# Five moves in the attention stage and one in the feed-forward stage of a fused kernel

## The chip, the cores and the metric

The kernel runs on one core of a Trainium2 chip. The metric is the device time of one execution in microseconds (us). The engines are TensorE (PE, with its weight loads as PEld), VectorE (DVE), ScalarE (ACT), GpSimd (POOL) and SyncE (SP, which here only issues DMAs). Each engine works through a queue of its own in order; semaphores tie the queues together.

## The reference

Three layers in float32: a linear attention with a decaying state, a gated top-1 mixture of experts with a skip, and a feed-forward layer.

```python
# attention: B, H, S, D = 4, 8, 768, 48
for t in range(S):
    state = alpha[:, :, t, :, None] * state + einsum('bhd,bhe->bhde', k[:, :, t], v[:, :, t])
    y[:, :, t] = einsum('bhd,bhde->bhe', q[:, :, t], state)
# mixture of experts: N = 3072 tokens, D = 384, E = 8 experts, F = 1024
do = x @ w_skip > 0
e = argmax(x[do] @ w_gate); gate = softmax(x[do] @ w_gate)[e]
out[do] = x[do] + gate * (relu(x[do] @ w1[e]) @ w2[e])
# feed-forward: d_ff = 2048
h = out @ w_in
return (h - tanh(h)) @ w_out
```

## The kernel before, in words

**Attention.** The sequence is cut into 24 units u (6 chunks of 128 steps for each of 4 batch entries, the batch entry running fastest). For each unit VectorE makes two scans over the decays `it`: `F` (running product from the start of the chunk, `scanF`, L196) and `G` (the same from its end, `scanG`, L203). `scanF` ends with a reciprocal that writes the four initial values of `G` into a tile `d1s[u % 2]` in SBUF, which is zero elsewhere; `scanG` reads that tile as its second operand. Then `qh` = q times F on GpSimd (L209), `kh` = k times G on VectorE (L214), and `pf`, a few factors for the state, on GpSimd (L221). TensorE makes the scores `pa` (`mmA`, L229; one PSUM buffer of two banks), VectorE masks them into `am` (`mask`, L234), and TensorE makes `py` from the state (`mmYs`) and from `am` (`mmYa`), transposes `kh` (`trk`) and updates the state (`mmS`). `evx`, `mmX` and `evxa` transpose the result into rows and compute the nine logits.

The order is written by hand. `astep(s)` issues, for step s: the loads of units s+4 and s+3, `mmA(s)`, `evx(s-2)`, the scans and `qh`, `pf` of unit s+2, `mmYs(s-1)`, `trk(s)`, `mmX(s-2)`, `mask(s)`, `mmYa(s-1)`, then `scanG` and `kh` of unit s+2, then whatever the lists `at[s]` and `aft[s]` hold, and `mmS(s)`. So scans run two units ahead of the scores.

**Routing.** The tokens are routed in three batches of 12, 8 and 4 units. For batch c, `route1` (argmax and so on, 13 small VectorE operations) and `route2` (counts by matmul, at the end of the step) come two steps after the batch's last unit, and `evr` and `route3` (the row addresses `loc`) one step later. Then `scatter(u)` writes the rows of one unit to DRAM (`xb`) with an indirect DMA of GpSimd: two in each of steps 15 to 20 for the first batch. `rload(0)` (issued at step 21) reads the first 512 token rows back.

**Weights.** A float32 weight tile is split into two parts for TensorE by `wsplit`. For the feed-forward weights that is four pieces, s0 (two VectorE operations), s1 (one VectorE, two ScalarE), s2 (two VectorE) and s3 (one VectorE). Five of them (NE0) are split during the attention steps, four steps apart, and the last five (NLATE) in the feed-forward loop itself: the pieces of weight k in steps 2k, 2k, 2k+1, 2k+1, all ahead of the step's own work.

**After the attention.** A tail routes the last batch and starts the feed-forward of the first 512 tokens on the five early weights (`mm1b`: h, then tanh, g, gh, gl; `mm2b`: y, two steps behind). Then 64 expert steps, then the feed-forward loop: 11 steps that finish the first 512 tokens with the remaining weights, and 80 steps for the other five blocks.

Of the kernel before, what the change touches and what calls it, by code (L numbers as in the profile page):

```python
# [9 lines left out]
F32 = mybir.dt.float32  # L10
# [51 lines left out]
def tile_kernel(ctx: ExitStack, tc: tile.TileContext, att0, att, vt, wsg, wmoe, wff, out):  # L62
# [47 lines left out]
    def flat(t_):  # L110
        return t_.rearrange("p a t -> p (a t)")
# [80 lines left out]
    def scanF(u):  # L192

        d = U[u]
        d["F"] = w2.tile([PR, NP, C], F32, tag="F", name=f"F{u}")
        V.tensor_tensor_scan(flat(d["F"]), d["it"][:, :NP * C], flat(ind), 0.0, ALU.mult, ALU.add)  # L196
        V.reciprocal(d1s[u % 2][:, :, C - 1:C], d["F"][:, :, C - 1:C])

    def scanG(u):

        d = U[u]
        d["G"] = w2.tile([PR, NP, C], F32, tag="G", name=f"G{u}")
        V.tensor_tensor_scan(flat(d["G"])[:, ::-1], d["it"][:, 1:NP * C + 1][:, ::-1], flat(d1s[u % 2])[:, ::-1], 0.0,  # L203
                             ALU.mult, ALU.add)

    def mkqh(u):
        d = U[u]
        d["qh"] = w2.tile([PR, NP, C], F32, tag="qh", name=f"qh{u}", bufs=4)
        G.tensor_tensor(d["qh"], d["qq"], d["F"], ALU.mult)  # L209

    def mkkh(u):
        d = U[u]
        d["kh"] = w2.tile([PR, NP, C], F32, tag="kh", name=f"kh{u}", bufs=3)
        V.tensor_tensor(d["kh"], d["kk"], d["G"], ALU.mult)  # L214

    def mkpf(u):
        d = U[u]
# [68 lines left out]
    def evx(u):  # L286
        d = U[u]
        d["xT"] = rt.tile([PR, NP, C], F32, tag="xT", name=f"xT{u}")
        A.copy(d["xT"], d["py"])

    def mmX(u):

        d = U[u]
        d["px"] = ps["T"].tile([128, NP, 128], F32, tag=f"X{u % 2}", name=f"px{u}")
        for p in range(NP):
            T.matmul(d["px"][:, p, :XW], d["xT"][:, p], selw[:, p], start=p == 0, stop=p == NP - 1)  # L296

    def evxa(u):
        k, i = where[u]
        r, n = RT[k], BATCHES[k]  # L300
        if i == 0:
            r["xr"] = rt.tile([128, n, RW], F32, name=f"xr{k}", bufs=1)
            r["l4"] = rt.tile([128, n, NP, 9], F32, name=f"l4{k}", bufs=1)
        A.copy(r["xr"][:, i, :DM].rearrange("p (a d) -> p a d", a=NP), U[u]["px"][:, :, :PD])
        A.copy(r["l4"][:, i], U[u]["px"][:, :, PD:XW])


    RT = [dict() for _ in BATCHES]
# [300 lines left out]
    ind = w1.tile([PR, NP, C], F32, name="ind")  # L609
    G.memset(ind, 0.0)  # L610
    G.memset(ind[:, :, 0:1], 1.0)
    d1s = [w1.tile([PR, NP, C], F32, name=f"d1_{i}") for i in range(2)]
    for t_ in d1s:
        V.memset(t_, 0.0)
    warm = cp.tile([128, 2], F32, name="warm")
    V.memset(warm, 1.0)
    A.activation(warm, warm, AF.Exp)
# [13 lines left out]
    zero = w1.tile([128, RW], F32, name="zero")  # L631
    scanF(0)
    mkqh(0)
    mkpf(0)
    scanG(0)
    mkkh(0)
    for t_ in pys:
        V.memset(t_, 0.0)
    G.memset(zero, 0.0)
# [19 lines left out]
    cnt4 = cp.tile([128, 1], F32, name="cnt4")  # L659
    scanF(1)  # L660
    mkqh(1)
    mkpf(1)
    scanG(1)
    mkkh(1)
    aload(2)
    for u in range(3):
        vload(u)
# [19 lines left out]
            xb[r0:r0 + 512, :].rearrange("(a p) d -> p a d", a=4), zero.unsqueeze(1).to_broadcast([128, 4, RW])))  # L687
    for k in range(NE0):
        at[max(1, 4 * k)].append(lambda k=k: wload(NMU + k))
        for s, f_ in zip((3 - k // 4, 4, 4, 6), wsplit(NMU + k)):  # L690
            aft[4 * k + s].append(f_)
    at[21].append(lambda: rload(0))
    for i in range(BATCHES[0]):
        aft[15 + i // 2].append(lambda i=i: scatter(i))

    def astep(s):

        def ok(u):
            return 0 <= u < NU

        def pX_(name):
            return ps["T"].tile([128, 512], F32, tag=f"X{s % 2}", name=name)

        if ok(s + 4):
            aload(s + 4)
        if ok(s + 3):
            vload(s + 3)
        for f_ in at[s]:
            f_()
        mmA(s)  # L710
        if ok(s - 2):
            evx(s - 2)
        c1 = next((k for k in range(len(BATCHES)) if s == first[k] + BATCHES[k] + 2), None)
        c3 = next((k for k in range(len(BATCHES)) if s == first[k] + BATCHES[k] + 3), None)
        if c3 is not None:
            evr(c3)
        if c1 is not None:
            route1(c1)
        if ok(s + 2):
            scanF(s + 2)  # L720
            mkqh(s + 2)
            mkpf(s + 2)
        if ok(s - 1):
            mmYs(s - 1)
        trk(s)
        if ok(s - 1):
            evst(s - 1)
        evk(s)
        if ok(s - 2):
            mmX(s - 2)  # L730
            evxa(s - 2)
        mask(s)
        if ok(s - 1):
            mmYa(s - 1)
        if c1 is not None:
            route1b(c1)
        if c3 is not None:
            route3(c3)
        if ok(s + 2):
            scanG(s + 2)  # L740
            mkkh(s + 2)
        for f_ in aft[s]:
            f_()
        mmS(s)
        if c1 is not None:
            route2(c1, pX_)
# [4 lines left out]
    ip_ctx.close()  # L751
    p0 = pool("p0", 1)
    rings["x2", 0] = p0
    for s in (NU - 2, NU - 1):
        a = 2 * (s - NU + 2)
        aft[s].append(lambda a=a: split2(0, a))
        astep(s)
        split2(0, a + 1)


    def pX(name):
        return ps["T"].tile([128, 512], F32, tag="X0", name=name)

    last = len(BATCHES) - 1
    mmYs(NU - 1)
    mmYa(NU - 1)
    evx(NU - 2)
    mmX(NU - 2)
    evxa(NU - 2)
    evx(NU - 1)  # L770
    att_ctx.close()
    rings["raw"] = pool("raws", 3, route_ctx, "right")
    part = p0.tile([128, 4, DM], F32, name="part")
    blk0 = ExitStack()
    rings["g"] = pool("g0", 3, blk0)
    i0, a0 = mm1b(0, 0, psS)
    i0(4)
    for u in range(first[1], first[last]):
        scatter(u)
    mmX(NU - 1)  # L780
    evxa(NU - 1)
    i0()
    for i in range(RING0):
        wload(i)
# [10 lines left out]
    evr(last)  # L795
    route1b(last)
    route3(last)
    for u in range(first[last], NU):
        scatter(u)
    psT_ctx.close()  # L800
# [50 lines left out]
    for e in range(1, NE):  # L851
        for a in range(2):
            aft[NF * e - 4 + a].append(lambda e=e, a=a: xprep(e, a))
        if e + 1 < NE:
            at[NF * e - 1].append(lambda e=e: xload(e + 1))
    at[20].append(lambda: rload(1))
    for i in range(NMU + 4):
        for f_ in at[i]:
            f_()
        if i < NMU:  # L860
            mm1(i)
        if 2 <= i < NMU + 2:
            mm2(i - 2)
        for f_ in aft[i]:
            f_()
# [3 lines left out]
    rings["x2", 1] = pool("p1", 1, ff_ctx, "right")  # L869
    rings["g"] = pool("g1", 2, ff_ctx, "right")  # L870
    steps = [(nb, f) for nb in range(NU // 4) for f in range(NF2) if nb or f >= NE0]
    at, aft = collections.defaultdict(list), collections.defaultdict(list)
    for k in range(NLATE):
        r = NMU + NF2 - NLATE + k
        at[max(0, 2 * k - 1 + 1)].append(lambda r=r: wload(r))
        for n, f_ in zip((0, 0, 1, 1), wsplit(r)):
            at[2 * k + n].append(f_)
    for nb in range(1, NU // 4):
        i = steps.index((nb, 0))
        for a in range(4):  # L880
# [4 lines left out]
    for i in range(len(steps) + 1):  # L885
        for f_ in at[i]:
            f_()
        if i < len(steps):
            issue, after = mm1b(*steps[i])
            issue()  # L890
            collections.deque(after(), 0)
        if 2 <= i < len(steps):
            mm2b(*steps[i - 2])
        elif i == len(steps):
            mm2b(steps[-1][0], *(f for _, f in steps[-2:]))
        for f_ in aft[i]:
            f_()
# [128 lines left out]
```

## Time and profile before

| what | value |
|---|---|
| median of 3 runs | 739.13 us (737.74 to 741.64) |
| the profiled execution | 738.44 us, of which the span of the profile is 736.8 us |
| attention with its last row copies | about 8 to 158 us |
| tail with the early feed-forward | about 158 to 181 us |
| expert steps | about 181 to 324 us |
| feed-forward on the late weights | about 324 to 379 us |
| the rest of the feed-forward | about 379 to 737 us |
| TensorE busy | 686.1 us (93%) |
| VectorE busy | 449.8 us (61%) |
| GpSimd busy | 125.3 us (17%) |

The times are read from one execution recorded by the hardware profiler. The shares are averages over stages that differ: each stage has to be read by itself. A wait is put down to the semaphore that came last by the profile.

### The profile page before, as it was taken

The page shows a single profiled execution, that of the slowest core. Times are in us where ns is not written, and L with a number is a line of the kernel's source. Part 1 is how long each engine was busy: PE and PEld are TensorE (multiplying, and loading weights), DVE is VectorE, ACT ScalarE, POOL GpSimd, SP SyncE. Part 2 cuts the span into 40 slices and gives each one's busy share as a digit, 9 for nine tenths or more (in the row PEclk, how much of TensorE's full clock was granted, in tenths as well). Part 3 has the DMA queues.
Part 4 walks back from the last instruction along what each step waited for, and adds up shares of the span by engine and source line. Part 5 has one row for each costly group of instructions (what it writes and reads, how often), then busy time and mean ns, then how long its engine had stood idle before and what let it go on. Part 6 is the DMA issues. An engine that isn't in the chain of part 4 may idle for free.

```text
span 736.8 us, 11897 instructions
## 1 busy us (share of the span) xinstructions
PE 686.1 (93%) x4707; PEld 629.2 (85%) x4707; DVE 449.8 (61%) x736; ACT 301.7 (41%) x588; POOL 125.3 (17%) x121
## 2 busy tenths in 40 slices
PE   3999978899999999999979999999999999999993
PEld 2888867788999999997768999999899999889892
DVE  8999999966888888847744334333333333333331
ACT  2546544345666656624422233233323333333220
POOL 5433347441011111210002001000200020001002
PEclk9999999899999999999989999999999999999997
DMA  9899957346779778512111001001100110001001
GB/s 275 180 218 281 230 145 219 98 155 207 253 257 321 257 249 268 168 64 85 45 44 43 1 1 61 25 1 44 43 1 1 45 43 1 1 1 43 2 1 46
DMA packets 30542, 81.39 MB, mean 110 GB/s; under 512 B 4405, under 2 KB 14677, under 8 KB 30480
## 3 DMA queue, kind: packets, MB, share of 16 engines
q1 hardware_dynamic: 26384, 68.64, 32.3%
q0 software_dynamic: 4096, 11.92, 4.4%
q8 instruction: 39, 0.64, 0.4%
q14 instruction: 23, 0.19, 0.1%
HBM read 65.45 MB, written 15.84 MB: 110 GB/s over the span
## 4 chain that ended last, share of the span: by engine, by line
issue 55%; PE 26%; DVE 12%; POOL 3%; ACT 1%; DMA 1%; POOLq 0%; ACTq 0%; SPq 0%; DVEq 0%
PE hp L560 8%; PE yp L578 3%; PE yp L579 3%; PE yp L580 3%; DVE G L203 2%; POOL out_dram L512 2%; DVE F L196 2%; PE pa L229 2%; DVE am L234 2%; PE py L243 2%; PE px L296 1%; PE h L464 1%; PE py L250 1%; DVE kh L214 1%; POOL qh L209 1%
## 5 line engine op out<-in xcount | busy, mean ns | idle before, releaser
L472 DVE TENSOR_TENSOR g<-h,g 128x512 f32<-128x512 f32 x96 | 66.3, 691 | 162.8 <-ACT g L470 162.8
L498 PE MATMUL y<-wh,gh 128*128 128x384 f32 x384 | 130.2, 339 | 0.7 <-ACT gh L474 0.7
L498 PE MATMUL y<-wh,gl 128*128 128x384 f32 x384 | 130.4, 340 | 0.2
L498 PE MATMUL y<-wl,gh 128*128 128x384 f32 x384 | 129.9, 338 | 0.0
L470 ACT ACTIVATE g<-h 128x512 f32<-128x512 f32 x96 | 57.3, 598 | 168.1 <-PE h L464 168.1
L464 PE MATMUL h<-xh,wh 128*128 128x512 f32 x288 | 116.2, 403 | 3.2 <-DVE g L472 3.1
L464 PE MATMUL h<-xh,wl 128*128 128x512 f32 x288 | 114.2, 397 | 3.6 <-DVE wl L170 3.6
L464 PE MATMUL h<-xl,wh 128*128 128x512 f32 x288 | 114.3, 397 | 0.0
L476 DVE TENSOR_TENSOR gl<-g,gh 128x512 fp32r<-128x512 f32 x96 | 66.5, 693 | 65.9 <-ACT gh L474 44.0
L474 ACT CAST gh<-g 128x512 fp32r<-128x512 f32 x96 | 59.5, 620 | 91.4 <-DVE g L472 91.4
L512 POOL DMA_INDIRECT out_dram<-ob,id x24 | 23.6, 983 | 375.8 <-DVE ob L511 308.0
L498 PEld LDWEIGHTS y<-wh,gh 128*128 128x128 f32 x384 | 72.4, 189 | 5.2 <-ACT gh L474 1.3
L498 PEld LDWEIGHTS y<-wl,gh 128*128 128x128 f32 x384 | 72.5, 189 | 4.2
L498 PEld LDWEIGHTS y<-wh,gl 128*128 128x128 f32 x384 | 72.3, 188 | 1.6 <-DVE gl L476 1.6
L464 PEld LDWEIGHTS h<-xh,wh 128*128 128x128 f32 x288 | 54.4, 189 | 14.5 <-DVE g L472 5.8
L464 PEld LDWEIGHTS h<-xh,wl 128*128 128x128 f32 x288 | 54.6, 190 | 12.5 <-DVE wl L170 3.9
L464 PEld LDWEIGHTS h<-xl,wh 128*128 128x128 f32 x288 | 54.5, 189 | 12.5
L141 ACT CAST wh<-raw 128x768 fp32r<-128x768 f32 x64 | 53.5, 835 | 24.1 <-PE yp L580 22.3
L144 DVE TENSOR_TENSOR wl<-raw,wh 128x768 fp32r<-128x768 f32 x64 | 60.8, 950 | 2.8 <-ACT wh L141 2.8
L560 PE MATMUL hp<-eh,wh 128*128 128x256 f32 x192 | 55.7, 290 | 1.3 <-DVE hl L565 1.3
L229 PE MATMUL pa<-qh,kh 64*128 64x128 f32 x384 | 30.8, 303 | 27.9 <-POOL qh L209 19.5
L560 PE MATMUL hp<-eh,wl 128*128 128x256 f32 x192 | 53.8, 280 | 0.0
(140 smaller groups left out, 1164.5 us busy)
## 6 DMA issues: line engine op xcount, KB each, us to landing
raw<-in_wmoe_dram SPq DMA_DIRECT2D x64, 384.0 KB, 4.0
raw<-in_wff_dram SPq DMA_DIRECT2D x16, 768.0 KB, 5.3
it<-in_att_dram SPq DMA_DIRECT2D x40, 289.5 KB, 7.9
rows<-xb SPq DMA_DIRECT2D x6, 776.0 KB, 4.3
vt<-in_vt_dram SPq DMA_DIRECT2D x24, 192.0 KB, 5.6
xb<-zero SPq DMA_DIRECT2D x4, 776.0 KB, 7.3
xe<-xb SPq DMA_DIRECT2D x8, 388.0 KB, 4.9
it<-in_att_dram SPq DMA_DIRECT2D x2, 772.0 KB, 8.5
```

The costliest lines, as they stand in the source:

```text
L141: A.copy(t_["h"], raw_t[i])
L144: V.tensor_tensor(t_["l"], raw_t[i], t_["h"].bitcast(F32), ALU.subtract)
L229: T.matmul(d["pa"][:, j, p], d["kh"][r, p], d["qh"][r, p], start=p == 0, stop=p == NP - 1)
L464: T.matmul(hp, *todo.pop(0), start=len(todo) == last, stop=not todo)
L470: A.activation(g, hp, AF.Tanh)
L472: V.tensor_tensor(g, hp, g, ALU.subtract)
L474: A.copy(gh, g)
L476: V.tensor_tensor(gl, g, gh.bitcast(F32), ALU.subtract)
L498: T.matmul(o, g_[:, sl_], w_[:, DM:], start=first and n == 0, stop=last and n == len(todo) - 1)
L512: s_ = nc.gpsimd.indirect_dma_start(out[:, :], bass.IndirectOffsetOnAxis(d["id"][:, a:a + 1], 0), ob, None, bounds_check=N - 1, oob_is_err ...
L560: T.matmul(hp, w_[:, ks], x_[:, k], start=n == 0, stop=n == 3 * KT - 1)
L578: T.matmul(o, hh[:, sl_], wh[:, DM:], start=f == 0, stop=False)
```

## The change

- `d1` is one tile in PSUM (a bank that is freed because `px` has one buffer X in place of X0 and X1).
- `kh` is computed on GpSimd. In a step the order becomes scanF, qh, scanG, kh, pf and later mask; `scanG` moves ahead of `mask`, and `pf` behind `kh`.
- The first two batches are routed one step sooner, `route1` and `route1b` now behind `mask` and `route3` of the step, and the first batch's scatters are laid over steps 14 to 20. The second batch's scatters come at step 23.
- The fifth early weight is split in steps 22 and 23 and in the tail (pieces s2 and s3).
- In the tail the last unit's `py` is copied by VectorE and its `px` takes half of the score buffer; four h matmuls that stood between the last two units go behind them.
- The late weights' pieces are laid over steps 2k-1 and 2k, two of them (`mid`) between the cast gh and the subtraction gl of the step.

```diff
-        V.reciprocal(d1s[u % 2][:, :, C - 1:C], d["F"][:, :, C - 1:C])
+        V.reciprocal(d1[:, :, C - 1:C], d["F"][:, :, C - 1:C])
...
-        V.tensor_tensor_scan(flat(d["G"])[:, ::-1], d["it"][:, 1:NP * C + 1][:, ::-1], flat(d1s[u % 2])[:, ::-1], 0.0,
+        V.tensor_tensor_scan(flat(d["G"])[:, ::-1], d["it"][:, 1:NP * C + 1][:, ::-1], flat(d1)[:, ::-1], 0.0,
...
-        V.tensor_tensor(d["kh"], d["kk"], d["G"], ALU.mult)
+        G.tensor_tensor(d["kh"], d["kk"], d["G"], ALU.mult)
...
-        A.copy(d["xT"], d["py"])
+        (V.tensor_copy if u == NU - 1 else A.copy)(d["xT"], d["py"])
...
-        d["px"] = ps["T"].tile([128, NP, 128], F32, tag=f"X{u % 2}", name=f"px{u}")
+        d["px"] = (ps["T"].tile([128, NP, 128], F32, tag="X", name=f"px{u}") if u < NU - 1 else
+                   ps["T"].tile([128, 2, NP, C], F32, tag="A", name=f"px{u}")[:, 0])
...
+        A.copy(r["l4"][:, i], U[u]["px"][:, :, PD:XW])
         A.copy(r["xr"][:, i, :DM].rearrange("p (a d) -> p a d", a=NP), U[u]["px"][:, :, :PD])
-        A.copy(r["l4"][:, i], U[u]["px"][:, :, PD:XW])
...
-    d1s = [w1.tile([PR, NP, C], F32, name=f"d1_{i}") for i in range(2)]
-    for t_ in d1s:
-        V.memset(t_, 0.0)
+    d1 = ps["T"].tile([PR, NP, C], F32, tag="D", name="d1")
+    V.memset(d1, 0.0)
...
-        for s, f_ in zip((3 - k // 4, 4, 4, 6), wsplit(NMU + k)):
-            aft[4 * k + s].append(f_)
+        early = wsplit(NMU + k)
+        for s, f_ in zip((3, 4, 4, 6), early):
+            if k < NE0 - 1:
+                aft[4 * k + s].append(f_)
...
-        aft[15 + i // 2].append(lambda i=i: scatter(i))
+        aft[14 + 7 * i // BATCHES[0]].append(lambda i=i: scatter(i))
...
-        c1 = next((k for k in range(len(BATCHES)) if s == first[k] + BATCHES[k] + 2), None)
-        c3 = next((k for k in range(len(BATCHES)) if s == first[k] + BATCHES[k] + 3), None)
+        c1 = next((k for k in range(len(BATCHES)) if s == first[k] + BATCHES[k] + 1), None)
+        c3 = next((k for k in range(len(BATCHES)) if s == first[k] + BATCHES[k] + 2), None)
...
-        if c1 is not None:
-            route1(c1)
         if ok(s + 2):
             scanF(s + 2)
             mkqh(s + 2)
+            scanG(s + 2)
+            mkkh(s + 2)
             mkpf(s + 2)
...
-        if c1 is not None:
-            route1b(c1)
         if c3 is not None:
             route3(c3)
-        if ok(s + 2):
-            scanG(s + 2)
-            mkkh(s + 2)
+        if c1 is not None:
+            route1(c1)
+            route1b(c1)
...
+    aft[NU - 1].append(lambda: [scatter(u) for u in range(first[1], first[last])])
     for s in (NU - 2, NU - 1):
         a = 2 * (s - NU + 2)
         aft[s].append(lambda a=a: split2(0, a))
+        aft[s].append(early[s - NU + 2])
         astep(s)
...
+    evx(NU - 2)
     mmYs(NU - 1)
     mmYa(NU - 1)
-    evx(NU - 2)
+    evx(NU - 1)
     mmX(NU - 2)
     evxa(NU - 2)
-    evx(NU - 1)
+    mmX(NU - 1)
+    evxa(NU - 1)
+    early[2]()
...
-    i0(4)
-    for u in range(first[1], first[last]):
-        scatter(u)
-    mmX(NU - 1)
-    evxa(NU - 1)
     i0()
...
     route3(last)
+    early[3]()
...
+    late = [wsplit(NMU + NF2 - NLATE + k) for k in range(NLATE)]
+    at[NMU + 1].append(lambda: wload(NMU + NF2 - NLATE))
+    at[NMU + 3].append(late[0][0])
...
-        r = NMU + NF2 - NLATE + k
-        at[max(0, 2 * k - 1 + 1)].append(lambda r=r: wload(r))
-        for n, f_ in zip((0, 0, 1, 1), wsplit(r)):
-            at[2 * k + n].append(f_)
+        if k:
+            at[max(0, 2 * k - 3)].append(lambda k=k: wload(NMU + NF2 - NLATE + k))
+            at[2 * k - 1].append(late[k][0])
+        (mid[2 * k - 1] if k else at[0]).append(late[k][1])
+        at[2 * k].append(late[k][2])
+        mid[2 * k].append(late[k][3])
...
-            collections.deque(after(), 0)
+            for n, _ in enumerate(after()):
+                if n == 2:
+                    for f_ in mid[i]:
+                        f_()
```

## Rows read from the trace of the kernel before

**Rows 1.** Stretches: start:end length, busy us by engine (x instructions), granted clock, DMA.

```profile
8.20:43.20 35.00, 27.90 (x344) 25.21 (x344) 33.80 (x50) 17.47 (x45) 17.48 (x17) 1.00 0.93 219
43.20:81.20 38.00, 36.97 (x504) 34.80 (x504) 37.34 (x45) 21.80 (x59) 16.90 (x15) 1.00 1.00 244
81.20:140.00 58.80, 46.53 (x617) 42.69 (x614) 57.32 (x94) 27.38 (x74) 33.01 (x27) 0.99 0.68 177
140.00:157.70 17.70, 17.49 (x162) 15.58 (x162) 12.22 (x42) 5.39 (x15) 4.56 (x5) 0.85 0.30 89
323.90:378.90 55.00, 48.22 (x222) 40.54 (x221) 40.73 (x59) 21.32 (x35) 2.25 (x2) 0.94 0.24 78
```

**Rows 2.** TensorE's waits from 0 to 160 us: total us, times, longest.

```profile
PE pa L229 <- POOL qh L209: 19.5, 11, 3.3
```

**Rows 3.** Timeline around one such wait: start us, us, instruction, [idle before].

```profile
64.07 1.20 DVE L234 TENSOR_TENSOR am<-pa,maskT 128x1024 f32<-128x1024 f32 x1
64.07 1.27 POOL L209 TENSOR_TENSOR qh<-it,F 128x512 f32<-128x512 f32 x1 [4.40 <-PE py L250]
...
65.41 0.83 PE L229 MATMUL pa<-qh,kh 64*128 64x128 f32 x10 [0.97 <-POOL qh L209]
```

**Rows 4.** Groups of instructions: busy us, mean ns, idle before.

```profile
L472 DVE TENSOR_TENSOR g<-h,g 128x512 f32<-128x512 f32 x96 | 66.3, 691 | 162.8 <-ACT g L470 162.8
...
L476 DVE TENSOR_TENSOR gl<-g,gh 128x512 fp32r<-128x512 f32 x96 | 66.5, 693 | 65.9 <-ACT gh L474 44.0 <-PE y L498 22.0
...
L203 DVE TENSOR_TENSOR_SCAN G<-it,d 128x512 f32<-128x512 f32 x24 | 32.4, 1351 | 0.1
L209 POOL TENSOR_TENSOR qh<-it,F 128x512 f32<-128x512 f32 x24 | 31.6, 1315 | 61.2 <-DVE F L196 20.7 <-PE py L250 11.1 <-ACT st L284 6.9
...
L415 POOL DMA_INDIRECT xb<-xr,loc x24 | 29.4, 1225 | 21.7 <-DVE basecnt L409 12.0 <-issue 6.7 <-DVE cnt L408 1.8
L196 DVE TENSOR_TENSOR_SCAN F<-it,ind 128x512 f32<-128x512 f32 x24 | 29.2, 1218 | 0.9 <-DMA it<-in_att_dram 0.9
L234 DVE TENSOR_TENSOR am<-pa,maskT 128x1024 f32<-128x1024 f32 x24 | 28.7, 1197 | 0.0
...
L221 POOL TENSOR_TENSOR pf<-it,F 128x4 f32<-128x4 f32 x20 | 20.2, 1010 | 0.0
...
L214 DVE TENSOR_TENSOR kh<-it,G 128x512 f32<-128x512 f32 x24 | 17.5, 729 | 0.8
L156 DVE SCALAR_TENSOR_TENSOR ca<-raw,cs 128x768 uint32<-128x768 uint32 x16 | 15.3, 959 | 0.6
...
L159 ACT ACTIVATE cl<-raw 128x768 f32<-128x768 uint32 x16 | 14.8, 924 | 0.0
```

**Rows 5.** Timeline of the first unit, GpSimd and VectorE.

```profile
5.06 1.26 POOL L209 TENSOR_TENSOR qh<-it,F 128x512 f32<-128x512 f32 x1 [2.52 <-DVE F L196]
...
5.17 2.23 DVE L203 TENSOR_TENSOR_SCAN G<-it,d 128x512 f32<-128x512 f32 x1
```

**Rows 6.** Timeline of `route1` of the first batch: first and last of 13 instructions.

```profile
89.28 0.90 DVE L327 TENSOR_REDUCE lg<-l 128x108 f32<-128x432 f32 x1
...
92.47 0.19 DVE L351 CAST oa<-ac 128x12 bf16<-128x12 f32 x1
```

**Rows 7.** DMA issues: count, KB each, median us from issue to landing.

```profile
rows<-xb SPq DMA_DIRECT2D x6, 776.0 KB, 4.3
...
xb<-xr,loc POOLq DMA_INDIRECT x24, 4.3
```

**Rows 8.** Timeline: first pieces of two late weights, and TensorE at the last.

```profile
344.57 0.55 DVE L155 TENSOR_SCALAR cs<-raw 128x768 uint32<-128x768 uint32 x1
...
354.68 0.55 DVE L155 TENSOR_SCALAR cs<-raw 128x768 uint32<-128x768 uint32 x1
...
368.47 0.51 PE L464 MATMUL h<-xh,wh 128*128 128x512 f32 x1 [0.60 <-DVE g L472]
372.58 0.79 PE L464 MATMUL h<-xh,wl 128*128 128x512 f32 x1 [3.60 <-DVE wl L170]
```

More of the change, by code (lines that the diff above doesn't have):

```diff
@@ L633, in tile_kernel @@
     mkqh(0)
-    mkpf(0)
     scanG(0)
     mkkh(0)
+    mkpf(0)
     for t_ in pys:
@@ L661, in tile_kernel @@
     mkqh(1)
-    mkpf(1)
     scanG(1)
     mkkh(1)
+    mkpf(1)
     aload(2)
@@ L701, in pX_ @@
         def pX_(name):
-            return ps["T"].tile([128, 512], F32, tag=f"X{s % 2}", name=name)
+            return ps["T"].tile([128, 512], F32, tag="X", name=name)
         if ok(s + 4):
@@ L753, in tile_kernel @@
     rings["x2", 0] = p0
+    last = len(BATCHES) - 1
+    aft[NU - 1].append(lambda: [scatter(u) for u in range(first[1], first[last])])
     for s in (NU - 2, NU - 1):
@@ L761, in pX @@
     def pX(name):
-        return ps["T"].tile([128, 512], F32, tag="X0", name=name)
-    last = len(BATCHES) - 1
+        return ps["T"].tile([128, 512], F32, tag="X", name=name)
+    evx(NU - 2)
     mmYs(NU - 1)
     mmYa(NU - 1)
-    evx(NU - 2)
+    evx(NU - 1)
     mmX(NU - 2)
     evxa(NU - 2)
-    evx(NU - 1)
+    mmX(NU - 1)
+    evxa(NU - 1)
+    early[2]()
     att_ctx.close()
@@ L871, in tile_kernel @@
     steps = [(nb, f) for nb in range(NU // 4) for f in range(NF2) if nb or f >= NE0]
-    at, aft = collections.defaultdict(list), collections.defaultdict(list)
+    at, mid, aft = (collections.defaultdict(list) for _ in range(3))
     for k in range(NLATE):
-        r = NMU + NF2 - NLATE + k
-        at[max(0, 2 * k - 1 + 1)].append(lambda r=r: wload(r))
-        for n, f_ in zip((0, 0, 1, 1), wsplit(r)):
-            at[2 * k + n].append(f_)
+        if k:
[4 more added lines that the diff above has]
+        mid[2 * k].append(late[k][3])
     for nb in range(1, NU // 4):
```

## Prediction

> **What bounds the kernel now.** I read the stretches first [rows 1]. Between 8 and 140 us TensorE stands idle for 35.00 - 27.90 = 7.1, 38.00 - 36.97 = 1.0 and 58.80 - 46.53 = 12.3 us, 20.4 us together, while VectorE is busy 97% of the same 131.8 us. [...] So VectorE sets the attention stage, and 23.1 us is the most that relieving it can give. The late-weight stretch (323.9 to 378.9 us) has 6.8 us of idle TensorE and a clock of 0.94 (another 3.3 us), 10.1 us at most. The change edits nothing that runs in the expert steps or after 379 us.
>
> The waits say where the idle time falls: 19.5 us, eleven times, ahead of the score matmul pa [rows 2]. They name GpSimd's qh, but qh at that moment is of a unit two steps ahead. The timeline shows the mask beginning at the same instant as qh and ending 1.20 us later, and pa starting 0.14 us after that [rows 3]: pa has one buffer, and the mask must empty it. The real releaser is the mask, late because VectorE is behind.
>
> A step then, in sums. TensorE needs 36.97 / 7 = 5.28 us (504 matmuls are 7 steps of 72) [rows 1]. VectorE needs F 1.22, mask 1.20, G 1.35 and kh 0.73 = 4.50 us, and a weight split of two short and four long operations, 2 x 0.55 + 4 x 0.96 = 4.9 us [rows 4, 8], every fourth step: 1.2 more, 5.7 in all. Routing comes on top.
>
> **The change, part by part.**
>
> *kh to GpSimd, d1 to PSUM.* VectorE loses kh, 24 x 0.73 = 17.5 us. In the first unit G took 2.23 us because qh on GpSimd had begun 0.11 us before it [rows 5]; both read two operands from SBUF. The mask, with one operand in PSUM, runs 1.20 us beside a qh of 1.27 [rows 3], so neither delays the other. With d1 in PSUM, G has the mask's kind of operands, and its mean should fall to F's 1.22: 3.2 us over 24. VectorE's step becomes 5.7 - 0.73 - 0.13 = 4.8 us. The new kh starts when G ends and outlives the mask by a little, and F, which still reads two SBUF operands, waits for it; I put 0.2 us on that (0 if GpSimd is early, 1.0 as in rows 5 if it is late). 5.0 us is below TensorE's 5.28, so TensorE sets the plain steps.
>
> No row shows a scan with a PSUM operand read backwards. Below, it costs nothing: an elementwise operation over 128x512 takes 691 ns with a PSUM operand and 693 without [rows 4]. Above, I bound it by a doubling, 2.4 us. I take the lower end, being nearest in kind. [...] The sum goes by the rows.
>
> *What stays of the 23.1 us.* Routing: route1 takes 92.47 + 0.19 - 89.28 = 3.4 us [rows 6]. It moves into the step in which its last logits are made, about two thirds into the step (3.5 us) plus 0.4 us of copies; the counts by matmul close that same step on TensorE. 3.5 + 0.4 + 3.4 = 7.3 us against 5.28: TensorE waits 2.0 us and with the lateness of VectorE some 2.5, for two batches 5.0. Queued behind it on TensorE is the next pa.
>
> GpSimd: a plain step is qh 1.3, kh 1.3 and pf 0.2 to 1.0, at most 3.6 of 5.28 us. Over steps 14 to 20 come 12 scatters of 1.23 plus 0.3 issue, 2.6 us a step: 5.4 to 6.2 us. It falls behind by up to 6 us, which the two-step lead of qh and kh absorbs, but the last scatter comes late. From its issue the landing (4.3) and the load of the first rows behind it (4.3) [rows 7] make 8.6 us, and step 22 transposes those rows: I put 2.5 us on that wait. At the start, F, G and kh of the first units still follow one another: half of the first stretch's 7.1 us stays, 3.5. Two steps with 1.9 us of split pieces overrun: 1.0. Together 12.0, so the attention gives 23.1 - 12.0 = 11.1 us.
>
> *One X bank and the earlier l4 copy.* px is copied out by ScalarE within the step that makes it, well before the next step's px, so I cost this at nothing; without that cover it would be a 0.5 us wait a step. More loads come no sooner than their buffers fall free; SP's queue issues in the same order.
>
> *Tail.* The fifth early weight puts s2 (1.9 us, half hidden behind the last px) ahead of route1 and s3 (0.96) ahead of the first g, on a chain that VectorE sets: +1.3 us net of the freed ScalarE copy. The second batch's scatters leave a queue that would stand before the last batch's, but GpSimd is done with them in time either way: 0. The four h matmuls only change places.
>
> *Late weights.* The first pieces of two weights stand 10.11 us apart, five weights at this pace [rows 8]; TensorE needs 2 x (48.22 - 3.3) / 11 = 8.2 us for two of the 11 steps. In the ten, VectorE waits twice 0.7 us for the cast gh. The pieces now placed there (s1's 0.55, s3's 0.96) fill that, -1.4 us; but the row transposes' copy now queues on ScalarE behind cl and wh (0.92 and about 0.8 [rows 4]), and VectorE's half waits for it, +0.7. A pair becomes 9.4; four pairs give 2.9 us. The last weight is done one step earlier, so the 3.60 us wait at 372.58 goes, and with it the drop of the clock that it brought, 3.3 us. The first g comes behind s2, +1.0. Sum: 2.9 + 3.6 + 3.3 - 1.0 = 8.8 us, of 10.1 at most and some 5 if a pair gains nothing but the last wait shrinks.
>
> *Sum.* The profiled execution took 738.44 us (span 736.8; the median of the runs is 0.7 above it). 738.4 - 11.1 + 1.3 - 8.8 = 719.8, forecast 720.
>
> **The rivals.**
>
> *GpSimd becomes the bound (17%).* For: 5.4 to 6.2 us a step against 5.28 over seven steps, and each late qh or kh holds up a two-operand VectorE operation by up to 1.0 us. Against: 33.01 of 58.80 us busy now [rows 1], and the lead of two steps. Price: 7 steps x 1.1 us = 8 us of the 11.1: 728. [...]
>
> *The scan pays for PSUM (5%), the other side.* If G takes 2.4 us, VectorE's step is 6.2, above the 5.7 of before: 20 steps x 0.5 = 10 us lost where 11.1 were to be won. 738.4 + 10 + 1.3 - 8.8 = 741. From about 2.2 us a scan the attention loses more than the late weights give. Against: the PSUM rows above.
>
> *The late weights gain nothing (8%).* The pieces are the same work on the same engine; if the filled waits reappear elsewhere, pairs stay at 10.1 and the last wait stays: 729. Against: the finishing step is one earlier by construction.
>
> *Both of the first and third (3%)*: 737, no change.
>
> **How the numbers follow.** The forecast holds 67%, by itself 712 (attention 17, late weights 10) to 727. With GpSimd's 728 and the 729 of the third rival the range 711 to 729 leaves out less than 2 in 10. A change of 0.5% (3.7 us) is about what can be told from none: faster 0.92 (67 + 17 + 8), same 0.03, slower 0.05.
>
> **What would show it.** G near 1.22 us with no long ones; kh on POOL near 1.3; pa's waits down from 19.5 to under 9 us, the largest two at the steps that route; the last attention matmul near 147 us; no wait on wl in the late steps, their pieces 9.4 us apart, and a clock of 1.00 there. Wrong would be: pa waiting for kh on GpSimd in steps 16 to 22, F or the splits stretched to 2 us beside it, G over 2 us, or a routing wait long enough to drop the clock (3.3 us of idling was followed by a drop before [rows 1, 2]; each costs some 2.7).

## The result: 0.985 of the time before, about what the late weights give alone

The changed kernel takes 727.79 us (median of 4 runs, 726.72 to 728.02), the kernel before, beside it, 739.27 us (737.74 to 741.64): ratio 0.9851, 95% interval 0.9829 to 0.9873. Run again on another occasion it took 725.9 us (725.67 to 726.19), ratio 0.9831 (0.9812 to 0.985). The forecast was 720, the range 711 to 729. So the sign and the range held, and the forecast was 6 to 8 us too low. The question is where these went.

The stretches of the changed kernel, with the columns of [rows 1]:

```profile
8.20:43.20 35.00, 29.07 (x348) 26.38 (x346) 32.07 (x41) 17.65 (x45) 22.84 (x24) 0.95 0.91 217
43.20:81.20 38.00, 36.85 (x504) 34.49 (x500) 34.05 (x38) 22.27 (x60) 22.27 (x21) 1.00 0.98 247
81.20:140.00 58.80, 48.59 (x626) 45.29 (x628) 56.97 (x98) 26.18 (x73) 42.72 (x37) 0.94 0.73 186
140.00:157.70 17.70, 16.96 (x157) 15.14 (x155) 12.28 (x34) 6.79 (x18) 8.04 (x8) 0.90 0.43 139
323.90:378.90 55.00, 53.47 (x267) 47.18 (x266) 42.76 (x64) 23.30 (x39) 1.92 (x2) 1.00 0.24 78
```

Read the last row first. In the late-weight stretch TensorE is busy 53.47 of 55.00 us at a clock of 1.00, where [rows 1] had 48.22 at 0.94. That is the gain that was forecast. Then the third row: VectorE is still full, 56.97 of 58.80 us where it was 57.32, although `kh` has left it, and TensorE's clock has fallen from 0.99 to 0.94. By landmarks: the score matmul `pa` of step 13 begins at 81.30 us (before 81.24), the first `h` after the attention at 155.56 (before 155.40, with four of the 18 `h` matmuls of that weight placed ahead of a break of 1.3 us), the first `h` of the late loop at 323.00 (before 323.94). About 0.9 us of the span's 10.6 were there when the late loop began; the other 9.7 come from it and what follows.

That the attention ends no sooner in this execution has two halves. From `pa` of step 15 to that of step 21 it takes 98.88 to 130.86, 31.98 us where it took 37.34 (95.23 to 132.57): 5.4 us are won in the steps between the routing steps. The routing steps 13 and 21, each with the step behind it, take 17.58 + 15.31 = 32.9 us where they took 13.99 + 15.14 = 29.1: 3.8 us are given back.

TensorE's waits from 0 to 160 us (total, times, longest), beside [rows 2]:

```profile
PE pr L376 <- DVE oa L352: 8.7, 2, 4.4
PE pa L229 <- DVE am L234: 7.7, 5, 3.0
```

The wait of 19.5 us ahead of `pa` fell to 7.7, now under the name of the mask `am`, its real releaser. In exchange, 8.7 us stand in two waits ahead of `pr`, the counts of the routing. Together 16.4. The first of the two, in step 13, which begins at 81.30:

```profile
84.90 0.19 ACT L305 COPY l<-px 128x36 f32<-128x36 f32 x1 [0.23 <-PE px L297]
...
85.22 1.22 DVE L203 TENSOR_TENSOR_SCAN G<-it,d 128x512 f32<-128x512 f32 x1
...
86.36 1.20 DVE L234 TENSOR_TENSOR am<-pa,maskT 128x1024 f32<-128x1024 f32 x1
...
87.48 0.90 DVE L328 TENSOR_REDUCE lg<-l 128x108 f32<-128x432 f32 x1
...
91.00 0.27 PE L376 MATMUL pr<-oa,tri 128*128 128x130 bf16 x1 [4.35 <-DVE oa L352]
```

The batch's last logits are copied 3.8 us into the step, but `route1` begins at 87.48, 6.2 us into it: when they are there, VectorE has just ended the step's F, and G and the mask still stand ahead.

The groups of the attention over the whole execution (busy us, mean ns, idle before), beside [rows 4]:

```profile
L196 DVE TENSOR_TENSOR_SCAN F<-it,ind 128x512 f32<-128x512 f32 x24 | 33.9, 1411 | 6.0 <-DMA it<-in_att_dram 5.5 <-issue 0.5
...
L214 POOL TENSOR_TENSOR kh<-it,G 128x512 f32<-128x512 f32 x24 | 31.4, 1310 | 4.2 <-DVE G L203 2.2 <-PE py L243 1.1 <-PE px L297 0.9
...
L203 DVE TENSOR_TENSOR_SCAN G<-it,d 128x512 f32<-128x512 f32 x24 | 29.3, 1220 | 1.0
```

G costs 1220 ns and `kh` on GpSimd 1310, both as predicted. F went from 1218 to 1411, and it waited 5.5 us for loads of `it` where it had waited 0.9.

The same execution in step 21, where F is longest:

```profile
130.17 1.28 POOL L209 TENSOR_TENSOR qh<-it,F 128x512 f32<-128x512 f32 x1
...
130.63 3.12 DVE L196 TENSOR_TENSOR_SCAN F<-it,ind 128x512 f32<-128x512 f32 x1
...
131.40 1.27 POOL L214 TENSOR_TENSOR kh<-it,G 128x512 f32<-128x512 f32 x1
...
139.37 0.20 PE L376 MATMUL pr<-oa,tri 128*128 128x90 bf16 x1 [4.37 <-DVE oa L352]
```

GpSimd is late and its `qh` and `kh` fall on F. F ends at 133.75, 1.08 us after `kh` ends at 132.67: it got through only when both were done. Behind the wait of 4.37 us that follows, the 16 matmuls of the next `pa` take 1.85 us (granted clock 0.58 from 139.7 to 141.6 us) where in a plain step they take 1.16; behind the wait of 4.35 they take 2.08 (0.50 from 91.8 to 95 us).

### The profile page after: what moved, and what is told of

Same layout as the page of the kernel before. It is cut to its first block, busy times and chain, and to the rows that moved or that the text cites. A ratio compares the mean times of both kernels' runs of the same rounds, so it can differ in the third digit from the quotient of the medians.

```text
span 726.2 us, 11897 instructions
## 1 busy us (share of the span) xinstructions
PE 684.0 (94%) x4707; PEld 629.9 (87%) x4707; DVE 441.7 (61%) x712; ACT 301.0 (41%) x587; POOL 146.1 (20%) x145
## 4 chain that ended last, share of the span: by engine, by line
issue 53%; PE 26%; DVE 11%; DMA 4%; POOL 3%; ACT 2%; SPq 0%; POOLq 0%; DVEq 0%; ACTq 0%
PE hp L561 8%; DMA it<-in_att_dram 4%; PE yp L579 3%; PE yp L580 3%; PE yp L581 3%; DVE F L196 2%; POOL out_dram L513 2%; PE pa L229 2%; PE py L243 2%; PE px L297 1%; DVE G L203 1%; DVE am L234 1%; PE py L250 1%; DVE wl L144 1%; DVE ca L167 1%
## 5 line engine op out<-in xcount | busy, mean ns | idle before, releaser
L561 PE MATMUL hp<-el,wh 128*128 128x256 f32 x192 | 53.7, 280 | 0.0
```

What stands on the lines that cost most here:

```text
L561: T.matmul(hp, w_[:, ks], x_[:, k], start=n == 0, stop=n == 3 * KT - 1)
```

## The experiments

All were timed beside the kernel before, in four groups, each on a chip of its own: the first four, the next four (from "changed, again"), the next three, and the last. The times of before range from 737.9 to 742.5 us over these chips (0.6%), so kernels of different groups are compared by their ratio to before; 0.001 is 0.74 us. The intervals reach about 0.002 to either side, so a difference of two kernels is uncertain by some 0.003, 2 us.

| kernel | median us | ratio | 95% interval |
|---|---|---|---|
| late weights alone | 728.5 | 0.9873 | 0.9852 to 0.9893 |
| changed, routing's timing undone | 722.98 | 0.9792 | 0.9775 to 0.981 |
| changed, fifth buffer for vt | 724.16 | 0.9805 | 0.9787 to 0.9823 |
| changed, kh on VectorE | 731.21 | 0.9901 | 0.9884 to 0.9918 |
| changed, again | 725.9 | 0.9831 | 0.9812 to 0.985 |
| fifth buffer, routing undone | 724.12 | 0.98 | 0.9778 to 0.9821 |
| fifth buffer, kh on GpSimd to unit 16 | 723.11 | 0.9796 | 0.9774 to 0.9818 |
| fifth buffer, pf on VectorE | 724.01 | 0.9809 | 0.979 to 0.9829 |
| late weights and d1 in PSUM | 722.95 | 0.9796 | 0.9777 to 0.9816 |
| these and kh on GpSimd | 728.24 | 0.986 | 0.9835 to 0.9886 |
| fifth buffer, order F, mask, G | 726.45 | 0.9832 | 0.981 to 0.9854 |
| late weights, d1 in PSUM, order F, G, kh, mask | 738.12 | 0.9929 | 0.9904 to 0.9953 |

**The late weights alone.** The kernel before with the three hunks from `late = [wsplit(...)]` to the end of the diff, nothing else.

```diff
+    late = [wsplit(NMU + NF2 - NLATE + k) for k in range(NLATE)]
...
+        (mid[2 * k - 1] if k else at[0]).append(late[k][1])
+        at[2 * k].append(late[k][2])
+        mid[2 * k].append(late[k][3])
```

> The kernel before with the spreading of the late weights alone, nothing else of the change. In the profile after, the last h of the late loop (NLATE units) starts 10.4 us sooner than before, but 0.9 us of that was there already when the late loop began (323.00 against 323.94 us), so 9.4 to 9.5 us came in the loop itself. Theory (the change is worth what the late weights are worth, the attention's edits give next to nothing): 739.3 - 9.4 = 729.9 us, 729.0 to 731.0, which leaves about 2 us of the 11.5 for all the rest. Rival (the late loop's gain leans on the earlier edits, or these give several us that the landmarks hide): 733 to 737 us.

Measured: 728.5 us. Its late stretch, with the columns of [rows 1]:

```profile
323.90:378.90 55.00, 53.56 (x270) 47.43 (x269) 42.97 (x65) 23.45 (x40) 2.08 (x3) 1.00 0.23 78
```

The stretch is that of the changed kernel. The late weights give 0.0127, 9.4 us. All other parts together give 0.0022 to 0.0042 (the two ratios of the changed kernel), 1.6 to 3.1 us, where the prediction had 9.8.

**The routing's timing undone.** The changed kernel with batches routed a step later, as before.

```diff
-        aft[14 + 7 * i // BATCHES[0]].append(lambda i=i: scatter(i))
+        aft[15 + i // 2].append(lambda i=i: scatter(i))
...
-        c1 = next((k for k in range(len(BATCHES)) if s == first[k] + BATCHES[k] + 1), None)
-        c3 = next((k for k in range(len(BATCHES)) if s == first[k] + BATCHES[k] + 2), None)
+        c1 = next((k for k in range(len(BATCHES)) if s == first[k] + BATCHES[k] + 2), None)
+        c3 = next((k for k in range(len(BATCHES)) if s == first[k] + BATCHES[k] + 3), None)
...
+        if c1 is not None:
+            route1(c1)
         if ok(s + 2):
             scanF(s + 2)
...
+        if c1 is not None:
+            route1b(c1)
         if c3 is not None:
             route3(c3)
-        if c1 is not None:
-            route1(c1)
-            route1b(c1)
```

> The changed kernel with the routing's timing undone: both batches routed one step later, the scatters with it, and route1 again ahead of the step's scan; all else as changed. Theory T1 (the two waits of TensorE for the routing, 4.35 and 4.37 us, and the cold steps behind them, about 1.9 us each, are lost time that the earlier routing made): these go in part or whole, 5 to 10 us faster than the changed kernel, 718 to 723 us. Theory T3 (VectorE is full from 81 to 140 us in either order, 56.97 of 58.8 us, and the waits of TensorE are only where its slack shows): the end of attention stays, 726.5 to 729.5 us. What the prediction held (a later routing costs about 2 times 2 to 4 us more than the earlier one): 731 to 735 us.

Measured: 722.98 us, which looked like theory T1. But the profile said otherwise: step 13, the same code up to there, began at 78.26 us where the changed kernel's began at 81.30, without the wait of 3.04 us at step 5. Hence the changed kernel was run again, and this edit was tried once more on another base (both below).

**A fifth buffer for vt.**

```diff
-        U[u]["vt"] = w2.tile([128, H, D], F32, tag="vt", name=f"vt{u}", bufs=4)
+        U[u]["vt"] = w2.tile([128, H, D], F32, tag="vt", name=f"vt{u}", bufs=5)
```

> The changed kernel with a fifth buffer for vt, so that the load of vt three units ahead no longer holds up SP's queue until TensorE is through with the unit before, and the load of it behind it goes out about a step sooner. Theory T2 (the load of it came late for step 5 because of where it stood in SP's queue; in the changed kernel the DMA engines are nearly idle from 18 to 22 us, while SP waits): the waits of VectorE for it (2.9 us) and the wait of 3.04 us of pa at 35.98 go, and with them the slow clock behind: 3 to 4.5 us faster, 723.3 to 724.8 us, the step starts from 36 to 81 us that much sooner. Rival (the DMA engines are the limit there, share 0.95 to 1.06): the wait moves to the next load, 727.1 to 728.5 us. Second rival (gained by 81 us, given back where VectorE is full): the starts at 81 us are sooner, the end is not, 727 to 728.5 us.

Measured: 724.16 us. The issues on SP's queue (start, us), in the changed kernel:

```profile
19.79 0.35 SPq L190 DMA_DIRECT2D vt<-in_vt_dram  x1
20.18 0.43 SPq L125 DMA_DIRECT2D raw<-in_wff_dram  x1
20.72 0.83 SPq L185 DMA_DIRECT2D it<-in_att_dram  x2
```

and with the fifth buffer:

```profile
14.13 0.42 SPq L190 DMA_DIRECT2D vt<-in_vt_dram  x1
14.60 0.43 SPq L125 DMA_DIRECT2D raw<-in_wff_dram  x1
16.04 0.99 SPq L185 DMA_DIRECT2D it<-in_att_dram  x2
```

The load of `it` goes out 4.7 us sooner, F waits 1.3 us for loads in place of 5.5, and step 13 begins at 77.42 us. Theory T2 holds in its mechanism: the load was late because of the load of `vt` ahead of it in the queue. Its size is smaller than expected against the second run of the changed kernel: 0.0026, 1.9 us, no more than the uncertainty.

**kh back on VectorE.**

```diff
-        G.tensor_tensor(d["kh"], d["kk"], d["G"], ALU.mult)
+        V.tensor_tensor(d["kh"], d["kk"], d["G"], ALU.mult)
```

> The changed kernel with k's decay (kh) back on VectorE, the initial values still in PSUM, the new order of the four operations kept. Theory T3 (on GpSimd it takes from VectorE by holding up its scans and splits what it gave back in work: from 81 to 140 us 6.2 us of kh removed, F's mean 1219 to 1607 ns over 9, so 3.5 us, and about 3.3 us more on the splits' wl, cs): F is back at 1.22 us, VectorE as full as before, 726.5 to 729.5 us. What the prediction held (the move is worth about 0.5 to 0.7 us a step where VectorE is full, 12 steps): 733 to 736 us.

Measured: 731.21 us, 0.0050 to 0.0070 slower than the changed kernel, 3.7 to 5.2 us. Between the two expectations, and T3 does not hold as it was put: in the order of the change, the move to GpSimd is worth its price, though F is held. The landmarks say where. With `kh` on VectorE step 13 begins at 84.14 us, in the kernel with the routing undone, the changed kernel's code up to there, at 78.26 and in the second run of the changed kernel (below) at 78.95; from there to the first `h` the three take 74.44, 74.71 and 74.71 us. So the move's 5 us lie in the first 13 steps, and between 81 and 140 us, where T3 was about, it gives nothing.

**The changed kernel again**, as measure for the next three.

> The changed kernel itself once more, as the measure for the runs beside it. Its first 13 steps are the same code as those of the kernel with the routing's timing undone, whose profile had no wait of 3.04 us at step 5 and reached step 13 at 78.26 us where the changed kernel's reached it at 81.30. If the late load of it belongs to the changed kernel: 726.7 to 728.3 us again, and the stall in the profile. If it comes and goes with the execution or the chip: 723 to 725 us, no stall, step 13 near 78.3 us, and the routing's timing is then worth nothing.

Measured: 725.9 us, between the two expectations; step 13 at 78.95 us, the wait at step 5 1.03 us. The long stall of the first profile comes and goes with the execution; 4.3 us of F's waits for `it` remain. From step 13 to the first `h` this run takes 153.66 - 78.95 = 74.71 us and the kernel with the routing undone 152.97 - 78.26 = 74.71: the same.

**Fifth buffer and routing undone.**

> The changed kernel with the fifth buffer for vt and with the routing's timing undone as well. Theory T3 (VectorE's fill between 81 and 140 us sets the end; from step 13 to the first h the changed kernel took 74.26 us and the one with the routing undone 74.71 us): the same as with the fifth buffer alone, 724.2, so 723.4 to 725.2 us. Theory T1 (the earlier routing is what costs, 4.8 us by the medians): 719 to 720.5 us.

Measured: 724.12 us, 0.98 against 0.9805. T1 falls: where the loads are in time, the routing's timing is worth nothing. What stands in place of the two waits is a wait for the mask in ten steps, and one for the first rows (TensorE, 0 to 160 us):

```profile
PE pa L229 <- DVE am L234: 11.6, 10, 2.2
...
PE px L438 <- DMA rows<-xb: 2.5, 1, 2.5
```

Without the fifth buffer the two medians, of different groups, stand 2.9 us apart (0.9792 against 0.9831) though the profiled executions agree (725.1 and 725.79 us); whether up to 3 us hang on the routing there is open. With the routing undone the fifth buffer gives nothing either: 0.9792 without it, 0.98 with it.

**kh on GpSimd for units 0 to 16 only.**

```diff
-        G.tensor_tensor(d["kh"], d["kk"], d["G"], ALU.mult)
+        (G if u < 17 else V).tensor_tensor(d["kh"], d["kk"], d["G"], ALU.mult)
```

> The changed kernel with the fifth buffer for vt, and kh on GpSimd for units 0 to 16 alone, on VectorE for units 17 to 23 (made in steps 15 to 21, where GpSimd also sends the scatters). Theory T3 (where two scatters a step are on GpSimd it runs late, 5.5 to 5.9 us a step, its kh and qh fall on VectorE's F and splits and hold them): F back at 1.22 us in steps 15 to 21, 4.5 us of stretch gone for 7 times 0.7 = 4.9 us of kh on VectorE, the waits of pa shorter; net 0 to 3 us faster than the fifth buffer alone: 721 to 724.2 us. Rival (the work itself, not the stretch, fills VectorE): 724.2 to 727 us.

Measured: 723.11 us, 0.9796 against 0.9805: 0.7 us less, inside the intervals. Between 81 and 140 us:

```profile
L196 DVE TENSOR_TENSOR_SCAN F<-it,ind 128x512 f32<-128x512 f32 x8 | 9.7, 1215 | 0.0
...
L214 DVE TENSOR_TENSOR kh<-it,G 128x512 f32<-128x512 f32 x7 | 5.7, 812 | 0.7
```

The stretch of F is gone, and the 5.7 us of `kh` take its place. In these steps the two are worth about the same.

**pf on VectorE.**

```diff
-            G.tensor_tensor(d["pf"], d["it"][:, NP * C + 1:NP * C + 1 + NP], d["F"][:, :, C - 1], ALU.mult)
+            V.tensor_tensor(d["pf"], d["it"][:, NP * C + 1:NP * C + 1 + NP], d["F"][:, :, C - 1], ALU.mult)
```

> The changed kernel with the fifth buffer for vt, and pf (four columns) on VectorE in place of GpSimd. Theory T3: GpSimd is freed of 0.5 to 1.1 us a step and is no longer late (5.0 to 5.2 us a step where 5.28 are there), so F falls from 1.6 towards 1.25 us between 81 and 140 us, 3 us, for 14 times 0.18 = 2.5 us on VectorE, of which half lies where it is not full: 1 to 3 us faster than the fifth buffer alone, 721 to 723 us. Rival (VectorE is full, and F's stretch stays): 724.5 to 726.7 us.

Measured: 724.01 us, no difference. F's mean between 81 and 140 us is 1584 ns where it is 1656 with the fifth buffer alone: freeing GpSimd of its smallest operation does not bring it back into time. The expected gain was not there.

The next runs build the change up from the other end, from the late weights:

**Late weights and d1 in PSUM.** One `d1` and one X bank, `kh` on VectorE, order and routing as before.

```diff
-        d["px"] = ps["T"].tile([128, NP, 128], F32, tag=f"X{u % 2}", name=f"px{u}")
+        d["px"] = ps["T"].tile([128, NP, 128], F32, tag="X", name=f"px{u}")
...
-    d1s = [w1.tile([PR, NP, C], F32, name=f"d1_{i}") for i in range(2)]
-    for t_ in d1s:
-        V.memset(t_, 0.0)
+    d1 = ps["T"].tile([PR, NP, C], F32, tag="D", name="d1")
+    V.memset(d1, 0.0)
```

> The kernel before with the late weights spread and d1 in PSUM (one buffer, and one X bank in place of two), kh on VectorE and all else of the attention as before. By ratio the late weights alone stand at 0.987. Theory (G costs VectorE 0.13 us less a step and nothing else changes; VectorE is full for about 12 steps): 1.2 to 2.8 us faster, ratio 0.9835 to 0.9855, 726 to 727.5 us where before is 739. Rival (with one X bank TensorE waits for ScalarE's copies, or VectorE's slack takes it): ratio 0.987 to 0.989.

Measured: 722.95 us, 0.9796: 0.0077 or 5.7 us from this edit alone, twice the upper end of what was expected, and less time than the whole change takes. Between 81 and 140 us (busy us, mean ns):

```profile
L415 POOL DMA_INDIRECT xb<-xr,loc x12 | 12.9, 1074 | 4.4 <-issue 2.3 <-DVE cnt L408 1.8 <-DVE G L203 0.3
...
L203 DVE TENSOR_TENSOR_SCAN G<-it,d 128x512 f32<-128x512 f32 x9 | 10.9, 1208 | 0.0
...
L214 DVE TENSOR_TENSOR kh<-it,G 128x512 f32<-128x512 f32 x9 | 6.2, 692 | 0.3
...
L221 POOL TENSOR_TENSOR pf<-it,F 128x4 f32<-128x4 f32 x5 | 1.0, 210 | 0.0
```

No long G is left, and GpSimd gains too: `pf`, which ran beside G, takes 210 ns where its mean was 1010 [rows 4]. The first `pa` begins 0.9 us sooner than with the late weights alone (7.26 against 8.20), the second 1.8 sooner (14.54 against 16.36), step 13 2.4 sooner, the first `h` 5.3 sooner (149.02 against 154.32). The part up to the second step is G's and its followers' at the start, half of which the prediction had set down as staying.

**These and kh on GpSimd**, in the order F, mask, G.

> The one with the late weights and d1 in PSUM, with kh on GpSimd as well; the order on VectorE (F, mask, G) and the routing's timing as before. From the changed kernel the move of kh was worth 5 us by ratio (0.9901 against 0.9831). If it is worth the same here: ratio 0.977 to 0.980, 722 to 724.5 us, the best part of the change without the rest. Rival (in this order kh on GpSimd falls on VectorE's splits or next F in every step, so F is stretched as from 81 to 140 us in the changed kernel): F's mean over 1.5 us in all steps, ratio 0.983 to 0.989.

Measured: 728.24 us, 0.0064 or 4.7 us slower: the rival by its ratio, but not by its sign. F's mean is 1346 ns over the attention, not over 1500 in all steps; what stretches most is the split's `ca`, 17.2 us for ten where they take 9.6. `kh` now starts beside the pieces of the weight split. In this kernel:

```profile
100.92 0.54 DVE L155 TENSOR_SCALAR cs<-raw 128x768 uint32<-128x768 uint32 x1
...
101.15 1.46 POOL L214 TENSOR_TENSOR kh<-it,G 128x512 f32<-128x512 f32 x1 [3.10 <-DVE G L203]
...
101.49 1.93 DVE L156 SCALAR_TENSOR_TENSOR ca<-raw,cs 128x768 uint32<-128x768 uint32 x1
```

and in the one with `kh` on VectorE:

```profile
102.04 0.69 DVE L214 TENSOR_TENSOR kh<-it,G 128x512 f32<-128x512 f32 x1
...
102.65 0.55 DVE L155 TENSOR_SCALAR cs<-raw 128x768 uint32<-128x768 uint32 x1
...
103.24 0.96 DVE L156 SCALAR_TENSOR_TENSOR ca<-raw,cs 128x768 uint32<-128x768 uint32 x1
```

VectorE is rid of 0.69 us of `kh` and pays 0.97 on the `ca` that runs beside it, 1.93 us in place of 0.96: it begins 0.34 us behind `kh` and ends 0.81 us after it. Between 81 and 140 us 6.2 us of `kh` leave VectorE, and `ca` and F cost 4.8 and 2.1 us more. The loss comes late: step 18 begins at 113.06 us here and at 113.62 in the kernel with `kh` on VectorE. From 81.2 to 140 us GpSimd, with the scatters, is busy 42.75 of 58.80 us where it was 25.17 with `kh` on VectorE, and one `ca` takes 3.69 us:

```profile
118.97 3.69 DVE L156 SCALAR_TENSOR_TENSOR ca<-raw,cs 128x768 uint32<-128x768 uint32 x1
119.32 1.28 POOL L209 TENSOR_TENSOR qh<-it,F 128x512 f32<-128x512 f32 x1
120.55 1.27 POOL L214 TENSOR_TENSOR kh<-it,G 128x512 f32<-128x512 f32 x1
...
136.96 2.08 PE L229 MATMUL pa<-qh,kh 64*128 64x128 f32 x16 [3.49 <-DVE am L234]
```

The `pa` of step 22 is slow behind a wait of 3.49 us, TensorE then waits 1.53 us for the first rows, and step 23 begins at 146.28 us in place of 141.33.

**Fifth buffer and the order F, mask, G**, all else as changed.

```diff
             mkqh(s + 2)
-            scanG(s + 2)
-            mkkh(s + 2)
             mkpf(s + 2)
...
             mmYa(s - 1)
+        if ok(s + 2):
+            scanG(s + 2)
+            mkkh(s + 2)
```

> The changed kernel with the fifth buffer for vt and VectorE's order of before: F, then the mask, then G, where the change has F, G, mask. Theory (G ahead of the mask is what keeps TensorE waiting for am, 7.5 us in 6 waits in the second run of the changed kernel): these waits go, 2 to 4 us faster than the fifth buffer alone (ratio 0.9805), ratio 0.975 to 0.978. Rival (VectorE is full, the order moves the wait and nothing else): 0.980 to 0.982. Second rival (kh on GpSimd now runs beside F and holds it): slower, 0.983 to 0.988.

Measured: 726.45 us, 0.0027 or 2.0 us slower, about the uncertainty: the second rival, at its lower end. The waits for the mask fall, as the theory had it, but those for the routing grow from 7.8 to 10.6 us: `kh` on GpSimd takes 1567 ns in the mean (36 to 140 us), and it is the splits on VectorE more than F that it holds (the two `wl` between 81 and 140 us take 2084 ns, F 1210). So with `kh` on GpSimd the change's order, which puts it beside the mask, costs nothing; if anything it is the better one.

**Late weights, d1 in PSUM, and the change's order with kh on VectorE**, since two kernels with `kh` on VectorE stood 0.0105 apart. The edit is the one above in reverse.

> The kernel before with the late weights spread, d1 in PSUM, kh on VectorE, and the change's order on VectorE: F, G, kh, mask in place of F, mask, G, kh. Routing, tail and the fifth early weight as before. Two kernels with kh on VectorE and d1 in PSUM stand 7.8 us apart by ratio: 0.9796 with the order and the routing of before, 0.9901 with the change's. Theory O (the order is the cost: G and kh, 1.9 us, stand ahead of the mask that frees pa's buffer, so each step that VectorE fills makes TensorE wait for am): ratio 0.987 to 0.990, 728.5 to 731 us, waits of pa for am over 12 us. Rival (the routing a step sooner, the tail and the fifth weight cost it): ratio 0.979 to 0.982, 723 to 725 us.

Measured: 738.12 us where before took 742.5 beside it: 0.0133 or 9.8 us slower than without the new order. Theory O, and by more than expected:

```profile
PE pa L229 <- DVE am L234: 21.9, 13, 4.4
```

With the order F, mask, G the same wait, there put down to `qh`, is 15.8 us. G and `kh`, 1.9 us, stand ahead of the mask that empties `pa`'s one buffer. Step 13 begins at 82.87 us in place of 78.72, the first `h` at 158.39 in place of 149.02, 9.4 us later.

## Why the forecast was 6 to 8 us too low, step by step

Laid end to end by ratio, one way from before to the changed kernel's second run is:

| edit | us, of 739 |
|---|---|
| late weights spread | -9.4 |
| d1 in PSUM, one X bank | -5.7 |
| order F, G, kh, mask (kh on VectorE) | +9.8 |
| routing sooner, tail, fifth weight | -2.1 |
| kh to GpSimd | -5.2 |
| sum | -12.6 |

Each has some 2 us of uncertainty, from the two intervals that it stands between. And the prices of the order and of `kh`'s move hang on each other. Taken the other way round, `kh` to GpSimd in the order of before costs +4.7 us (0.9796 to 0.9860), and the new order with routing, tail and fifth weight then gives -2.1 (0.9860 to 0.9831). Both ways the two together, with routing, tail and fifth weight, lose 2.6 us of what `d1` in PSUM had won.

- *Late weights, -8.8 predicted, -9.4 measured.* Right in mechanism and size: the wait of 3.60 us for `wl` is 0.36, the clock 1.00. The first pieces of two weights stand 7.7 to 9.0 us apart, not 9.4 (the first two, of which one is now split ahead of the loop, 6.3).
- *The 23.1 us at most.* 20.4 of them are idle time of TensorE [rows 1]. The other 2.7, from its clock between 140 and 157.7 us, are a term that no run shows; the runs show a granted clock there of 0.85 before, 0.90 in the changed kernel and 0.96 in its second run, with TensorE busy 17.49, 16.96 and 16.96 of 17.70 us.
- *G without a price for PSUM.* Right: its mean is 1220 ns with one operand in PSUM, F's 1218 with both in SBUF [rows 4]. Its worth was mis-sized: the prediction counted VectorE's 3.2 us alone, and the edit by itself (with the one X bank, which was not run apart) gave 5.7.
- *kh to GpSimd for 0.2 us of F, and the new order at no price.* This is the step that failed: VectorE's step was to fall from 5.7 to 5.0 us, and the two edits were to bring most of the attention's 11.1. The order puts G, and `kh` where it is on VectorE, ahead of the mask that, by the prediction's own second paragraph, TensorE waits for. With `kh` still on VectorE that costs 9.8 us; with `kh` on GpSimd nothing is left of that cost, but the 0.2 us on F does not hold. Between 81 and 140 us F costs 9 x (1607 - 1219) ns = 3.5 us more, and the split's `wl` and `cs` about 3.3 more (five operations), 6.8 in nine steps or 0.75 a step. `kh` took 9 x 0.69 = 6.2 us away. So VectorE stayed full there, and the move's 5.2 us, all in the first 13 steps, undo part of what the new order cost.
- *"TensorE sets the plain steps".* Right between the routing steps: from step 15 to 20 four of the six take 5.27 to 5.28 us, the six together 32.0 where they took 37.3.
- *What stays: routing 2 x 2.5.* Mis-sized, and here the missing time shows. The waits are 4.35 and 4.37 us, since `route1` began not 3.9 us into its step, when its logits were there, but, the first time, 6.2, when VectorE came to it; and behind each the clock fell (0.50 and 0.58), which the prediction had named as a sign of being wrong. But the waits are only where VectorE's lateness came out: undoing the timing gave nothing on the fifth-buffer base, as it moves the wait to the mask and the first rows. The wait for the first rows, put at 2.5, came with the late routing alone (2.5 and 3.2 us).
- *Loads, "I cost this at nothing".* Wrong by 2 us at most: the load of `it`, queued behind that of `vt`, came late (4.3 and 5.5 us of F's waits in two executions), and a fifth buffer brought 1.9 us, or nothing with the routing undone.
- *The rival "GpSimd becomes the bound", 728.* The time fits, the mechanism only in part. In the steps with scatters GpSimd was all but full (32.44 of 35.00 us from 100 to 135 us), and F was held up to 3.12 us and `wl` up to 2.01, as its sign said. Yet TensorE was busy 33.60 of the same 35.00 us, so GpSimd did not set these steps, and taking the stretch away brought under 1 us, since it brought `kh` back to VectorE.
- *The signs.* G, `kh` on GpSimd, `pa`'s waits under 9 us and the clock of the late weights came as said. The last matmuls of the attention, put near 147 us, end where the first `h` begins, at 155.56. That the time fell inside the range owes much to the late weights, which came out as forecast; the attention gave 1.6 to 3.1 us of 9.8.

Of the tail and the fifth early weight nothing was run alone, and late weights with `d1` in PSUM were not run with the fifth buffer. As it is, that kernel (0.9796) is the simplest of those that stand near the lowest ratio here (0.9792), 2.6 us below the changed kernel's second run.

## What to carry to other kernels

Where one engine is full and another waits for one of its results, an edit's price is not only the work that it adds or takes away: ask what it puts ahead of that result. Work moved to another engine can come back as longer operations on the one that it left (here, in the order F, mask, G, 6.9 us on `ca` and F for 6.2 us of `kh` between 81 and 140 us), so choose what it will run beside. First try to shorten what is there: with one operand in PSUM G's mean fell from 1351 to 1208 ns, and `pf` beside it from 1010 to 231. When a change has several parts, time each alone and then in pairs: the order cost 9.8 us with `kh` on one engine and nothing with it on the other, so neither part has a price of its own.

## What the runs showed of the chip

- GpSimd's smallest operation, `pf` (four columns), takes 206 ns (mean from 36 to 140 us) and 231 (over the attention) in the kernel with the late weights and `d1` in PSUM, and 993 and 1010 in the kernel before, with both of G's operands in SBUF; the scatters' issue between 81 and 140 us takes 1074 ns there and 1438 before.
- Where GpSimd's `qh` and `kh` ran in a row beside one operation of VectorE, it took two to four times as long: F 3.12 us in place of 1.22 (changed kernel, step 21), `ca` 3.69 in place of 0.96 (late weights, `d1` in PSUM, `kh` on GpSimd). By the profile's starts the second of the two began after the operation that it held (`kh` 0.77 us after F), so the starts alone do not tell which of the two will be held.
- How long a single wait of TensorE was did not tell whether the next `pa` was slow: it took 2.07 and 2.24 us behind waits of 1.90 us (order F, G, kh, mask with `kh` on VectorE) and 1.52 (fifth buffer, order F, mask, G), and its 1.16 us right behind 2.59 (late weights and `d1` in PSUM), 2.66 (that kernel with the order F, G, kh, mask) and 3.04 (changed kernel, granted clock 1.00 from 36.0 to 37.1 us). Behind that last one the clock fell a little later: 0.71 from 37.1 to 42.9 us.
